# Values of attention: two head groups in one TensorE block, or one group at a time

## The chip, the cores and the metric

The kernel runs on one core of a Trainium2 chip. The metric is the device time of one launch in microseconds (us), the median of three runs. A core has five engines: TensorE (PE, with its weight loads shown apart as PEld), VectorE (DVE), ScalarE (ACT), GpSimd (POOL) and SyncE (SP). Each runs its own list of instructions in a fixed order and waits on semaphores for the others. Matmuls write to PSUM, of which this kernel uses all eight banks of 128 x 512 floats.

## The reference

Attention with normalised queries and keys over 8 batches, 12 heads, 448 tokens and 64 elements a head, and then a multiplicative feed-forward network (FFN) over the 3584 tokens:

```python
q_n, k_n = rmsnorm(q, g_q), rmsnorm(k, g_k)
scores = q_n @ k_n.T / sqrt(64)
attn = exp(scores - max) ; attn = attn / (sum(attn) + 1e-9)
x = (attn @ v) rearranged to [B * S, H * D]          # 3584 x 768
a = x @ w1 ; b = x @ w2                              # 768 -> 1024
out = ((a * b) @ w3) @ w_out                         # 1024 -> 1024 -> 768
```

The kernel leaves the maximum out, multiplies `w3` by `w_out` once (`w34`), and keeps the operands of its matmuls in bf16.

## The kernel before

The 96 heads are handled in 24 groups of four heads (`NQ = 24`, three groups a batch). For group `i` there are:

- preparation: squares on ACT, sums and scaling on DVE, transposition by TensorE (first five groups) or by DMA;
- seven score pieces (`NU = 7`): four 64x64 matmuls into two banks, then one `exp` of 128 x 896 on ACT, which writes `P` (six pieces) or `Pr` (the seventh);
- the values block: three kinds of 16 matmuls each, in 128x32 tiles. Kind 0 multiplies `P` by ones and gives the sums of the softmax, whose reciprocal ACT takes as exp(-ln); kinds 1 and 2 give the values, which DVE multiplies by the reciprocal into `xT`.

When the three groups of a batch are in `xT`, its FFN is pushed on a list as pairs: eight pairs of `x @ w1` or `x @ w2`, and three or four pairs of `(a * b) @ w34`, all in 64x64 tiles. A pair occupies two banks.

No order is written by hand. When the program is built, a planner steps through an estimated time and picks, whenever TensorE is free, what it does next; the order that comes out is fixed in the program. These are the parts that decide about scores and values (`r` is the time less a margin; `idle` are the free banks):

```python
    STOCK = 14
    PACE = 1.7
    # P: three buffers; the third lies in w_outs, once w34 is made
    p_bufs = [const.tile([NP, HQ, NF, S], BF, name="P" + str(z)) for z in range(2)]
    p_bufs.append(w_outs.rearrange("p c n -> p (c n)")[:, 0 : HQ * NF * S]. ...)

    def into(m):                       # DRAIN = 0.11 when the kind of tile changes
        extra = DRAIN if mode[0] != m else 0.0
        mode[0] = m
        return extra

    def score_ready(t):
        ...
        i, g = divmod(n, NU)
        if g == 0 and min(p_free(x) for x in range(3)) > t:
            return False
        stock = sum(p.name != "w" for p in waiting)
        if stock >= STOCK and t < last_score[0] + PACE:
            return False
        return max(qkT_at[i]) + SEM <= t

    def pv_ready(t):
        i = next_pv[0]
        if i >= NQ or all_of(p_at[i], NU) > t or landed[i]["v"] + SEM > t:
            return False
        ...
        if i % 2 or all_of(w34_at, CF) > t or i + 1 >= NQ:
            return True
        return all_of(p_at[i + 1], NU) <= t and landed[i + 1]["v"] + SEM <= t

    def pe_try(t, r):
        idle = idle_banks(r)
        if pv_state:                   # a values block that has begun goes on
            ...
        if mode[0] == "v" and len(idle) >= 1 and pv_ready(r):
            i = next_pv[0]             # the second group follows at once
            took = do_pv_kind(t, i, 0, single(idle))
            pv_state.append((i, 1))
            return took
        two = adjacent(idle)
        score = score_ready(r) and out_scores[0] < 2 and two is not None
        ...                            # the pair that runs goes on; turns; scores
        if late:
            return do_pass(late[0], t)
        want_pv = pv_ready(r)
        if want_pv and len(idle) >= 2:
            i = next_pv[0]
            took = do_pv_kind(t, i, 0, single(idle))
            pv_state.append((i, 1))
            return took
        if two is not None and new is not None and not want_pv:
            waiting.remove(new)
            start_pair(new, two)
            return do_pass(new, t)
```

Once `w34` is complete, an even group's values wait until the scores of the odd group after it have also passed the `exp`; then both groups' values run in one block of 96 matmuls.

Of the kernel before, what the change touches and what calls it, by code (L numbers as in the profile page):

```python
# [9 lines left out]
BF = mybir.dt.bfloat16  # L10
# [10 lines left out]
SEM = 0.05  # L21
# [24 lines left out]
class Planner:  # L46
# [11 lines left out]
    def add(self, *args, **kw):  # L58
        self.jobs.append(Job(*args, **kw))
# [136 lines left out]
def kernel(  # L196
# [15 lines left out]
    B, H, S, D = q.shape  # L212
    NP = 128
# [3 lines left out]
    NF = S // NP  # L217
    NU = 2 * NF + 1
    HQ = 4
    NQB = H // HQ  # L220
    NQ = B * NQB
    DM, DFF = moe_w1.shape
    CM = DM // 128
    CF = DFF // 128
# [5 lines left out]
    const = ctx.enter_context(tc.tile_pool(name="const", bufs=1))  # L230
    prep_pool = ctx.enter_context(tc.tile_pool(name="prep", bufs=3))
    qkT_pool = ctx.enter_context(tc.tile_pool(name="qkT", bufs=3))
    att_pool = ctx.enter_context(tc.tile_pool(name="att", bufs=2))
    p_pool = ctx.enter_context(tc.tile_pool(name="P", bufs=3))
    x_pool = ctx.enter_context(tc.tile_pool(name="x", bufs=3))
    ffn_pool = ctx.enter_context(tc.tile_pool(name="ffn", bufs=4))
    out_pool = ctx.enter_context(tc.tile_pool(name="outp", bufs=3))
# [7 lines left out]
    MARGIN = 0.25  # L245
    AHEAD_W3 = 4
    EARLY = 4
    STOCK = 14
    PACE = 1.7
    POOL_ORDER = (  # L250
        "w0 w1 o0 o1 q1 w2 w3 v0 q2 w4 w5 v1 w6 w7 v2 a0 a1 a2 q3 b0 v3 b1 q4 b2 q5".split()
# [4 lines left out]
    w2s = const.tile([128, CM, DFF], BF, name="w2s")  # L256
    w34s = const.tile([128, CF, DM], BF, name="w34s")
    w_outs = const.tile([128, CF, DM], BF, name="w_outs")
    p_bufs = [const.tile([NP, HQ, NF, S], BF, name="P" + str(z)) for z in range(2)]
    p_bufs.append(  # L260
        w_outs.rearrange("p c n -> p (c n)")[:, 0 : HQ * NF * S].rearrange(
            "p (h j s) -> p h j s", h=HQ, j=NF
        )
    )
    w3s = big_pool.tile([128, CF, DFF], BF, tag="big", name="w3s")
    w3T = big_pool.tile([128, CF, DFF], BF, tag="big", name="w3T")
    g_row = const.tile([1, 2, D], FP, name="g_row")
# [22 lines left out]
    landed = [{"q": INF, "k": INF, "v": INF} for _ in range(NQ)]  # L290
# [5 lines left out]
    p_at = [[] for _ in range(NQ)]  # L296
    pv_end = [INF] * NQ
    x_at = {b: [] for b in range(B)}
    x_used = [INF] * B
# [4 lines left out]
    w34_at = []  # L304
# [5 lines left out]
    def all_of(times, n):  # L310
        return max(times) if len(times) == n else INF
# [243 lines left out]
    mode = ["n"]  # L555

    def into(m):
# [4 lines that stand above are left out]
    def pass_us(n):  # L562
        return n / 2400 + 0.0025

    def idle_banks(t):
        return [z for z in range(8) if bank_at[z] <= t]

    def adjacent(idle):

        fit = [z for z in idle if z + 1 in idle]  # L570
        return min(fit, key=lambda z: (z % 2, z)) if fit else None

    def single(idle):

        return min(idle, key=lambda z: (z ^ 1 in idle, -z)) if idle else None
# [2 lines left out]
    last_score = [0.0]  # L578
    out_scores = [0]

    p_used = [None] * 3

    def p_free(x):

        if p_used[x] is None:
            return 0.0 if x < 2 else all_of(w34_at, CF)
        return pv_end[p_used[x]]

    def score_ready(t):
        n = next_score[0]  # L590
        if n >= NQ * NU:
            return False
        i, g = divmod(n, NU)
        if g == 0 and min(p_free(x) for x in range(3)) > t:
            return False
        stock = sum(p.name != "w" for p in waiting)
        if stock >= STOCK and t < last_score[0] + PACE:
            return False
        return max(qkT_at[i]) + SEM <= t

    def do_score(t, z):
        n = next_score[0]
        next_score[0] += 1
        last_score[0] = t
        i, g = divmod(n, NU)
        s = st[i]
        if g == 0:
            x = min(range(3), key=lambda x: (p_free(x) > t, x))
            s["P"] = p_bufs[x]
            p_used[x] = i  # L610
            s["Pr"] = p_pool.tile([NP, 2, S], BF, tag="Pr", name="Pr")
        took = pass_us(S) + into("n")
        qkT, sc = s["qkT"], ps_all[:, z : z + 2]
        for c in range(2):
            if g < 2 * NF:
                pr, blk = divmod(g, NF)
                j = blk if c == pr else J + blk
            else:
                pr, j = c, NF
            cols = slice(HP * pr, HP * pr + HP)  # L620
            for u in range(2):
                nc.tensor.matmul(  # L622
                    out=sc[HP * c : HP * c + HP, u, 0:S].rearrange(
                        "p (j s) -> p j s", j=NJ
                    ),
                    lhsT=qkT[u * D : (u + 1) * D, 1, j, cols],
                    rhs=qkT[u * D : (u + 1) * D, 0, :, cols],
                    start=True, stop=True, tile_position=(u * D, HP * c),
                )
        dst = (  # L630
            s["P"][:, pr::2, blk, :] if g < 2 * NF else s["Pr"]
        )
        bank_at[z] = bank_at[z + 1] = INF
        out_scores[0] += 1

        def done(e):
            bank_at[z] = bank_at[z + 1] = e + SEM
            out_scores[0] -= 1
            p_at[i].append(e + SEM)

        at = t + took + TO_ENGINE - pass_us(S) + 0.187
        add(
            "ACT", 0.80, QUAD * i + 1.8 * g,
            lambda: nc.scalar.activation(out=dst, in_=sc[:, :, 0:S], func=AF.Exp),  # L644
            needs=[lambda: at - 0.187], done=done,
        )
        if g == NU - 1:
            qkT_used[i] = t + took + 0.2
        return took

    next_pv = [0]
    pv_state = []

    def pv_ready(t):
        i = next_pv[0]
        if i >= NQ or all_of(p_at[i], NU) > t or landed[i]["v"] + SEM > t:
            return False
        b, m = divmod(i, NQB)
        if m == 0 and b >= 3 and x_used[b - 3] > t:
            return False  # L660
        if i % 2 or all_of(w34_at, CF) > t or i + 1 >= NQ:
            return True
        return all_of(p_at[i + 1], NU) <= t and landed[i + 1]["v"] + SEM <= t

    def do_pv_kind(t, i, kind, z):
        s = st[i]
# [354 lines left out]
    def any_turn(t, r, idle, n):  # L1021

        if not idle:
            return None
        if turns:
            i, w = turns[0]
            if scaled_at[i][w] <= r:
                turns.pop(0)
                return do_turn(t, i, w, single(idle))
        ready = [fc for fc in w3_turns if w_at["w3"][fc] + SEM <= r]  # L1030
        if ready and (len(ready) >= n or ready[-1] == CF - 1):
            if ready[0] - len(w34_at) < AHEAD_W3:
                return do_w3_turn(t, w3_turns.pop(0), single(idle))
        return None
# [6 lines left out]
    def pe_try(t, r):  # L1041
        idle = idle_banks(r)
        if pv_state:
            i, kind = pv_state[0]
            z = single(idle)
            if z is None:
                return None
            took = do_pv_kind(t, i, kind, z)
            pv_state.clear()
            if kind == 2:  # L1050
                next_pv[0] += 1
            else:
                pv_state.append((i, kind + 1))
            return took
        if mode[0] == "v" and len(idle) >= 1 and pv_ready(r):
            i = next_pv[0]
            took = do_pv_kind(t, i, 0, single(idle))
            pv_state.append((i, 1))
            return took
        two = adjacent(idle)  # L1060
        score = score_ready(r) and out_scores[0] < 2 and two is not None
        hungry = free["ACT"] <= t + 0.3 and out_scores[0] == 0
        if mode[0] == "t":
            took = any_turn(t, r, idle, 1)
            if took is not None:
                return took
        if running[0] and running[0].ready() <= r:
            if score and hungry:
                return do_score(t, two)
            return do_pass(running[0], t)  # L1070
        took = any_turn(t, r, idle, 2)
        if took is not None:
            return took
        new = next_pair(r)
        late = [p for p in pairs if p.ready() <= r]
        if score:
            left = [z for z in idle if z not in (two, two + 1)]
            if hungry or late or new is None or adjacent(left) is not None:
                return do_score(t, two)
# [12 lines that stand above are left out]
        return any_turn(t, r, idle, 1)  # L1092
# [10 lines left out]
    with tc.manual_schedule():  # L1103
# [66 lines left out]
        for name in POOL_ORDER:  # L1170
            what, x = name[0], int(name[1])
# [9 lines left out]
            else:  # L1181
                dst, src, key = (w1s, moe_w1, "w1") if what == "a" else (w2s, moe_w2, "w2")
# [36 lines left out]
```

## Time and profile before

| what | value |
|---|---|
| time, median of three runs | 363.51 us (362.82 to 363.65) |
| span of the profiled run | 361.6 us |
| TensorE matmuls busy | 348.5 us (96%) |
| weight loads busy | 224.1 us (62%) |
| ACT busy | 265.6 us (73%) |
| DVE busy | 204.1 us (56%) |
| values, 24 groups | 1152 matmuls, 352 ns each, in four singles and ten blocks of two |

A matmul's time in the profile is from its start to the end of its results; matmuls overlap, and four of them run side by side in different tiles. What a matmul costs is read from start to start: a set of four over 448 columns takes 0.189 us, over 384 columns 0.162 us. In a timeline, neighbouring instructions of one kind are merged: the first number is when the group starts, the second how long it lasts, and xN how many instructions it has.

### The profile page before, as it was taken

Reading aid. Unit: us, or ns where it says so; the run is one execution under the profiler, and the core shown is the slowest. Engines: PE = TensorE matmul, PEld = TensorE weight load, DVE = VectorE, ACT = ScalarE, POOL = GpSimd, SP = SyncE. Lnnn points to the kernel's source line nnn. Section 1 sums busy time; section 2 is a strip of 40 time slices with the busy share of each in tenths; the row PEclk is TensorE's granted clock in tenths of the full one; section 3 lists DMA queues with packets and bytes.
Section 4 is the critical chain, followed back from the end, with each engine's and each line's share of the span. In section 5 each row is a group of like instructions: output and inputs, shape, how many; then the busy total and the mean of one; then the engine's idle time right before and its main releaser. Section 6 shows DMA issues by size and latency. Waiting matters only on the chain.

```text
span 361.6 us, 16194 instructions
## 1 busy us (share of the span) xinstructions
PE 348.5 (96%) x7358; PEld 224.1 (62%) x7358; DVE 204.1 (56%) x288; ACT 265.6 (73%) x378; POOL 75.3 (21%) x132
## 2 busy tenths in 40 slices
PE   8789999999999999999999999999999999999984
PEld 3466666557665667666565666655656566666673
DVE  5278367988988788866739497855442311220210
ACT  4879989989999999987998799866974542112121
POOL 8167452400400422040041401305000000000000
PEclk9999999999999999999999999999999999999999
DMA  8999998788999699985499949928530006004115
GB/s 181 255 238 195 262 271 241 144 166 204 240 208 262 109 234 244 222 173 133 103 231 223 168 81 257 203 56 86 98 104 2 4 11 170 4 2 102 37 22 154
DMA packets 68200, 55.11 MB, mean 152 GB/s; under 512 B 44900, under 2 KB 61956, under 8 KB 68132
## 3 DMA queue, kind: packets, MB, share of 16 engines
q1 hardware_dynamic: 49744, 36.51, 43.1%
q0 software_dynamic: 18016, 16.92, 26.8%
q8 instruction: 57, 0.93, 1.1%
q10 hardware_dynamic: 372, 0.66, 0.6%
q14 instruction: 11, 0.09, 0.1%
HBM read 46.66 MB, written 11.01 MB: 159 GB/s over the span
## 4 chain that ended last, share of the span: by engine, by line
PE 90%; DMA 4%; POOL 2%; ACT 2%; issue 1%; DVE 0%; POOLq 0%; DVEq 0%
PE ps_all L758 64%; PE ps_all L675 16%; PE ps_all L622 9%; DMA w3s<-in_moe_w_dram 4%; PE ps_all L976 1%; ACT P L644 1%; PE ps_all L998 1%; ACT w_outs L644 0%; POOL w3s L388 0%; POOL w_outs L394 0%; POOL qk_sb L336 0%; DVE abT L841 0%; POOL v_sb L1118 0%; ACT Pr L644 0%; DVE o_sb L327 0%
## 5 line engine op out<-in xcount | busy, mean ns | idle before, releaser
L644 ACT ACTIVATE P<-ps_all 128x896 bf16<-128x896 f32 x120 | 104.1, 923 | 12.7 <-PE ps_all L622 12.0
L359 POOL DMA_DIRECT2D v_sb<-in_v_dram x96 | 57.1, 611 | 167.5 <-PE ps_all L675 114.2
L758 PE MATMUL ps_all<-xT,w2s 64*64 64x448 bf16 x1536 | 88.5, 349 | 0.1
L758 PE MATMUL ps_all<-xT,w1s 64*64 64x448 bf16 x1536 | 87.3, 349 | 0.0
L758 PE MATMUL ps_all<-w34s,abT 64*64 64x384 bf16 x1792 | 82.3, 323 | 1.3 <-DVE abT L841 1.3
L841 DVE TENSOR_TENSOR abT<-ps_all,a_sb 128x896 bf16<-128x896 f32 x32 | 34.9, 1090 | 78.9 <-PE ps_all L758 69.8
L758 PEld LDWEIGHTS <-abT 64*64 64x64 bf16 x1792 | 57.1, 107 | 18.6 <-issue 1.5
L417 DVE TENSOR_REDUCE ssq<-sq 128x14 f32<-128x896 f32 (+1 forms) x50 | 51.4, 1042 | 23.8 <-ACT sq L410 23.8
L622 PE MATMUL ps_all<-qkT 64*64 64x448 bf16 x672 | 60.2, 352 | 3.1 <-ACT P L644 2.0
L758 PEld LDWEIGHTS <-w2s 64*64 64x64 bf16 x1536 | 46.0, 107 | 26.8 <-POOLq L743 0.5
L758 PEld LDWEIGHTS <-w1s 64*64 64x64 bf16 x1536 | 45.9, 107 | 26.1 <-issue 0.6
L440 DVE TENSOR_TENSOR qks<-qk_sb,al 128x448 bf16<-128x448 f32 x96 | 55.6, 618 | 1.8 <-ACT al L429 1.6
L410 ACT ACTIVATE sq<-qk_sb 128x896 f32<-128x896 f32 (+1 forms) x50 | 45.3, 917 | 1.0 <-DMA qk_sb<-in_q_dram 0.9
L321 ACT ACTIVATE a_sb<-ps_all 128x896 bf16<-128x896 f32 x23 | 21.1, 916 | 28.4 <-PE ps_all L758 28.3
L710 DVE TENSOR_TENSOR xT<-ps_all,r 128x448 bf16<-128x448 f32 x48 | 27.7, 618 | 13.3 <-ACT r L691 13.3
L321 ACT ACTIVATE o_sb<-ps_all 128x768 f32<-128x768 f32 (+1 forms) x19 | 15.2, 798 | 24.6 <-PE ps_all L758 24.6
L622 PEld LDWEIGHTS <-qkT 64*64 64x64 bf16 x672 | 21.4, 106 | 17.9 <-issue 8.4
L675 PEld LDWEIGHTS <-v_sb 128*32 128x32 bf16 x768 | 20.6, 97 | 15.8
L675 PE MATMUL ps_all<-P,v_sb 128*32 128x448 bf16 x480 | 29.6, 352 | 0.0
L644 ACT ACTIVATE w_outs<-ps_all 128x896 bf16<-128x896 f32 x24 | 21.6, 914 | 6.7 <-PE ps_all L622 5.8
L758 PE MATMUL ps_all<-w_outs,w3T 64*64 64x384 bf16 x512 | 24.0, 324 | 0.7 <-DMA w_outs<-in_moe_w_out_dram 0.7
L644 ACT ACTIVATE Pr<-ps_all 128x896 bf16<-128x896 f32 x24 | 22.2, 924 | 3.0 <-PE ps_all L622 3.0
(55 smaller groups left out, 218.4 us busy)
## 6 DMA issues: line engine op xcount, KB each, us to landing
out_dram<-o_sb SPq DMA_DIRECT2D x55, 192.0 KB, 3.8
qk_sb<-in_q_dram SPq DMA_DIRECT2D x18, 448.0 KB, 4.8
qk_sb<-in_k_dram SPq DMA_DIRECT2D x18, 448.0 KB, 5.9
v_sb<-in_v_dram POOLq DMA_DIRECT2D x48, 64.0 KB, 4.8
v_sb<-in_v_dram POOLq DMA_DIRECT2D x48, 48.0 KB, 4.5
qk_sb<-in_q_dram POOLq DMA_DIRECT2D x5, 448.0 KB, 9.1
qk_sb<-in_k_dram POOLq DMA_DIRECT2D x5, 448.0 KB, 9.5
w3s<-in_moe_w_dram POOLq DMA_DIRECT2D x8, 256.0 KB, 5.9
```

Of the source, the lines that this page charges most:

```text
L321: nc.scalar.activation(out=out, in_=in_, func=AF.Copy, scale=1.0 if by is None else by)
L359: nc.gpsimd.dma_start(out=v_bufs[i % 4][p0 : p0 + HP, g::2, 0 : j1 - j0].rearrange("p h j d -> p h (j d)"), in_=src[:, g::2, j0:j1].rearra ...
L410: nc.scalar.activation(out=s["sq", t][:, x0:x1], in_=src[:, t, x0:x1], func=AF.Square)
L417: nc.vector.tensor_reduce(out=s["ssq"][:, t, x0:x1], in_=s["sq", t][:, x0:x1], axis=AX, op=ADD)
L440: nc.vector.tensor_tensor(out=s["qks"][:, t, :, x], in0=src[:, t, x], in1=s["alpha"][:, t, x].unsqueeze(2).broadcast_to([NP, NJ, D]), op=MULT,
L622: nc.tensor.matmul(out=sc[HP * c : HP * c + HP, u, 0:S].rearrange("p (j s) -> p j s", j=NJ), lhsT=qkT[u * D : (u + 1) * D, 1, j, cols], rh ...
L644: lambda: nc.scalar.activation(out=dst, in_=sc[:, :, 0:S], func=AF.Exp),
L675: nc.tensor.matmul(out=ps[hd * HALF : (hd + 1) * HALF, :], lhsT=w, rhs=s["P"][:, hd, j, :] if j < NF else s["Pr"][:, hd // 2, :], start=(j ...
L710: lambda: nc.vector.tensor_tensor(out=xT[b][:, 2 * m + kind - 1, :], in0=ps, in1=s["r"], op=MULT),
L758: mm = nc.tensor.matmul(out=ps_all[64 * h : 64 * h + 64, p.bank + z, 0 : p.n], lhsT=lhsT[64 * r : 64 * r + 64, 64 * h : 64 * h + 64], rhs= ...
L841: nc.vector.tensor_tensor(out=abT[bp][:, f0 : f0 + 2, odd * S : (odd + 1) * S], in0=ps_all[:, z : z + 2, 0:S], in1=a_sb[b, f0], op=MULT,)
L976: nc.tensor.transpose(ps[:, j], s["qks"][:, w, j].rearrange("p x d -> p (x d)"), ident)
```

## The change

The changed kernel gives up the block of two groups. Each group's values run on their own, as soon as its seven `exp` are done and the planner finds a place. The third `P` buffer in `w_outs` goes, `P` comes from a pool of two buffers, and the pool of `Pr` shrinks from three to two with it. The scores of group `i` may begin when the values of group `i - 2` have been taken. The stock of waiting FFN pairs from which scores are paced at 1.7 us falls from 14 to 10. The aim is a simpler order, in which values are taken as they come and `x` of a batch is complete earlier. The arithmetic and the number of matmuls stay the same.

```diff
-    p_pool = ctx.enter_context(tc.tile_pool(name="P", bufs=3))
+    p_pool = ctx.enter_context(tc.tile_pool(name="P", bufs=2))
...
-    STOCK = 14
+    STOCK = 10
...
-    p_bufs = [const.tile([NP, HQ, NF, S], BF, name="P" + str(z)) for z in range(2)]
-    p_bufs.append(
-        w_outs.rearrange("p c n -> p (c n)")[:, 0 : HQ * NF * S].rearrange(
-            "p (h j s) -> p h j s", h=HQ, j=NF
-        )
-    )
...
-    p_used = [None] * 3
-    def p_free(x):
-        if p_used[x] is None:
-            return 0.0 if x < 2 else all_of(w34_at, CF)
-        return pv_end[p_used[x]]
...  # score_ready
-        if g == 0 and min(p_free(x) for x in range(3)) > t:
+        if g == 0 and i >= 2 and pv_end[i - 2] > t:
             return False
...  # do_score
-            x = min(range(3), key=lambda x: (p_free(x) > t, x))
-            s["P"] = p_bufs[x]
-            p_used[x] = i
+            s["P"] = p_pool.tile([NP, HQ, NF, S], BF, tag="P", name="P")
             s["Pr"] = p_pool.tile([NP, 2, S], BF, tag="Pr", name="Pr")
...  # pv_ready
-        if m == 0 and b >= 3 and x_used[b - 3] > t:
-            return False
-        if i % 2 or all_of(w34_at, CF) > t or i + 1 >= NQ:
-            return True
-        return all_of(p_at[i + 1], NU) <= t and landed[i + 1]["v"] + SEM <= t
+        return m > 0 or b < 3 or x_used[b - 3] <= t
...  # pe_try
-        if mode[0] == "v" and len(idle) >= 1 and pv_ready(r):
-            i = next_pv[0]
-            took = do_pv_kind(t, i, 0, single(idle))
-            pv_state.append((i, 1))
-            return took
```

## The prediction

> **What bounds the kernel now.** I read the page's busy times and slices first, then the groups, then the chain in order of time, and last the timeline of TensorE around values blocks and around its few waits.
>
> ```profile
> PE 348.5 (96%) x7358; PEld 224.1 (62%) x7358; DVE 204.1 (56%) x288; ACT 265.6 (73%) x378; POOL 75.3 (21%) x132
> ...
> PE   8789999999999999999999999999999999999984
> ...
> ACT  4879989989999999987998799866974542112121
> PEclk9999999999999999999999999999999999999999
> ```
>
> TensorE is at nine tenths in every slice from the fifth to the last but one, at the full clock. ACT is as full for the first 24 slices (to about 217 us) and then falls off. So two engines are loaded early, TensorE alone late. A busy PE is not yet a PE at its peak, so I checked it by counting. From the groups by shape, in sets of four: 768 sets of the first FFN layer, 168 of scores and 288 of values at 0.189 us, 448 sets of the second layer and 128 for w34 at 0.162 us, 134 transposes at about 0.067 us: 145.2 + 31.8 + 54.4 + 72.6 + 20.7 + 9.0 = 333.7 us of pure streaming in a span of 361.6. The first score set starts at 11.6 us and the last matmul ends 5.4 us ahead of the end. Only about 12 us in between are lost. Taking start-to-start times less streaming, I find 5.5 us of it before 27 us (weights landing), 3.0 us at changes of tile, 1.4 us near 80 us, 0.9 us near 122 us and 1.4 us at 345.7 us. From 123 to 344 us TensorE does not wait once. **The end is set by how much TensorE has to do**, and what the change can win or lose is in the terms of a few microseconds just listed.
>
> The timeline of TensorE around the first block of two groups shows the price of a change of tile:
>
> ```profile
> 86.21 0.98 PE L758 MATMUL ps_all<-w34s,abT 64*64 64x384 bf16 x19
> 87.12 0.75 PE L675 MATMUL ps_all<-P,ones 128*32 128x448 bf16 x12
> 87.69 0.36 PE L675 MATMUL ps_all<-Pr,ones 128*32 128x448 bf16 x4
> 87.88 0.74 PE L675 MATMUL ps_all<-P,v_sb 128*32 128x448 bf16 x12
> ...
> 91.48 0.36 PE L675 MATMUL ps_all<-Pr,v_sb 128*32 128x448 bf16 x4
> 91.77 0.38 PE L622 MATMUL ps_all<-qkT 64*64 64x448 bf16 x4
> 91.98 1.31 PE L758 MATMUL ps_all<-w34s,abT 64*64 64x384 bf16 x28
> ```
>
> Inside the block a set follows the last after 0.19 us (87.69 to 87.88). From the block's last set to the next score it is 91.77 - 91.48 = 0.29 us: 0.10 us too long. At the entry, the last FFN set starts at 86.21 + 0.98 - 0.32 = 86.87 and the values at 87.12: 0.25 us where a set takes 0.16, so 0.09 us. Over all fourteen blocks the sum is 3.0 us, or 0.21 us a block.
>
> The same view before 82 us shows the one cluster of real waits in the middle:
>
> ```profile
> 79.36 0.55 PE L758 MATMUL ps_all<-xT,w2s 64*64 64x448 bf16 x8
> 79.74 0.55 PE L622 MATMUL ps_all<-qkT 64*64 64x448 bf16 x8
> 80.60 0.38 PE L622 MATMUL ps_all<-qkT 64*64 64x448 bf16 x4 [0.31 <-ACT P L644]
> 81.41 0.38 PE L622 MATMUL ps_all<-qkT 64*64 64x448 bf16 x4 [0.43 <-ACT P L644]
> 81.60 1.17 PE L758 MATMUL ps_all<-w34s,abT 64*64 64x384 bf16 x24
> ```
>
> The first FFN layer of batch 0 has ended at 79.7; its second layer can start only when DVE has made the last products; nothing is left but scores, and each score waits for an exp to free its banks. The groups show what one such wait is made of:
>
> ```profile
> L644 ACT ACTIVATE P<-ps_all 128x896 bf16<-128x896 f32 x120 | 104.1, 923 | 12.7 <-PE ps_all L622 12.0
> ```
>
> Scores can't come faster than one every 0.8 to 0.9 us, against 0.19 us of TensorE: three of them in a row lose 1.4 us. The same thing happens at 121.4 to 123.1 (0.9 us).
>
> **What the Trainium skill says.** "TensorEngine Tiling (Array Packing)", section Key Properties: changing the tiling mode, and not just the tile, drains TensorE. The trace agrees: about 0.10 us at each change between 64x64 and 128x32, nothing extra within one mode. "TensorE: Matmul & The Clock Gate", section "Wait — 56ns, not 53.3ns?": a warm matmul follows the last after N / 2.4 GHz plus some 2.5 ns; for 448 columns that is 189.2 ns, and the trace has 189. "Perfetto Trace Analysis", section Identifying the Most-Contended Engine, warns that matmul busy time is a bad measure, which is why I counted sets above rather than trust 96%.
>
> **The change part by part.**
>
> 1. *Blocks split.* The 24 groups are now in four singles and ten blocks of two, so 14 blocks. Afterwards nothing joins two groups, as the branch that let a second group follow at once is gone and a pass or a score will come between. That makes 24 blocks, ten more, each with one more entry and one more exit: 10 x 0.21 = **+2.1 us**, all on TensorE. Ahead of 123 us there are two or three of these, where they may fall into waits; the other seven or eight (1.5 to 1.7 us) hit a TensorE that never waits. I count the whole 2.1. A transpose ahead of values costs much the same at the entry (0.149 us start to start, of which 0.067 is streaming), so it is no matter what stands before a block.
>
> 2. *Values no longer wait for the partner.* An even group's values become ready about one group of scores, 7 to 15 us, sooner. Group 4 has its last score at 74.3 and its values only at 87.1; group 8 at 120.1 and 130.7. A values block is 12 x 0.189 = 2.27 us of work that needs no scarce ACT result, and is larger than each of the waits at 80 (1.4 us) and 122 us (0.9). If it falls there, both go: -2.3 us. But the planner takes ready values before it starts a new pair, so group 4's may be spent at 76 or 77 us, ahead of the hole, which then comes two microseconds later with the same shape. I give it a bit under half: **-0.9 us**. Batch 2 also has its x at about 124 instead of 135, which helps to refill the list; later the list is never empty, so nothing is won there.
>
> 3. *Two P buffers, not three.* The scores of group i + 2 now wait for the values of i. They were ready a whole group earlier, and a pair that runs delays them by at most some 2 to 5 us, less than the 7 exps of one group need (7 x 0.92 = 6.4 us). ACT may wait now and then, which matters only while TensorE has no stock, before 123 us. Up to 78 us the kernel before has only two buffers too (the third is in w_outs), with ACT 24.3 of 26 us busy from 52 to 78; between 92 and 118 it was 25.25 of 26. That 4% over some 40 us is 1.5 us of exp time, of which a part can return as wait: **+0.3 us**.
>
> 4. *STOCK 10.* A batch adds 11 or 12 pairs, two of which start at once. So scores are paced at 1.7 us a little after each push, and more once stock remains. It moves exps later, from where ACT is full to where it is half empty. From 291 us on TensorE has nothing but 64 us of FFN, so attention may end tens of microseconds later with no harm. **0 us**.
>
> 5. *Start and end.* The first 27 us don't touch the changed branches (no values before 27.1 us). The wait of 1.3 us for the last product at 345.7 and the 5.4 us after the last matmul belong to the order of the last batch, which stays: **0 us**.
>
> Sum: +2.1 - 0.9 + 0.3 = +1.5 us, 363.5 + 1.5 = **365.0 us**, 0.4% slower.
>
> **The rivals.** (a) *The holes are filled and all else stays*: 363.5 + 2.1 - 2.3 = 363.3 us. For it: the first values fit into the very hole at 80 us. Against it: the planner's preference for values ahead of new pairs. (b) *ACT becomes the bound early*: with two buffers and a lower stock, scores slow down, the FFN list runs dry at each batch's end, and a hole like that at 80 us (1 to 1.5 us) appears at two or three more batches: 363.5 + 2.1 + 3 = 368.6 us. For it: ACT at nine tenths to 217 us, and only two holes' distance from empty. Against it: values are never later, so the FFN of each batch is pushed sooner. (c) *The switches are hidden*, since values beside idle gaps cost nothing: then only the gains count and the time is 362 to 363 us. Against it: no wait at all between 123 and 344 us to hide them in.
>
> **Range and chances.** The low end takes all of the hole's gain and a little better refill (362.6); the high end takes the full switches, no gain and one more hole (367.8). All three rivals lie within 1.5%; 2% is 7.3 us, three times the switch cost, so a change by over 2% either way needs something I don't see. Faster 0.01, same 0.96, slower 0.03.
>
> **What would show it right or wrong.** In the timeline after: 24 blocks of 48 matmuls at line of the values matmul, each with about 0.09 us at entry and 0.10 at exit (step 1); no wait of TensorE for ACT's P near 80 and 122 us, or the same holes a few microseconds later (step 2); ACT's busy share from 92 to 118 us below 97% (step 3); the last values later than 288.5 us with fewer than 64 us of FFN after them (step 4); the wait for the last product still about 1.3 us (step 5). The prediction is wrong if blocks still abut, if TensorE waits in the stretch from 123 to 344 us, or if the final FFN is broken up by scores.

## The result, and the profile after

The changed kernel takes 366.88 us (median of six runs, 366.32 to 367.98); the kernel before took 363.06 beside it. The ratio is 1.0106, with a 95% interval from 1.0087 to 1.0126: 3.8 us, or 1.1%, slower. The ratios given here can differ by up to 0.0007 from the quotient of the two medians. The profiled run is the longest of the six, with 367.98 us and a span of 366.2.

The page of the changed kernel, busy times and slices:

```profile
PE 352.2 (96%) x7358; PEld 220.9 (60%) x7358; DVE 207.7 (57%) x292; ACT 264.7 (72%) x374; POOL 75.4 (21%) x132
...
PE   8799999999889999999999999999999999999984
...
ACT  4879989959969999997688669976796557122221
PEclk9999999999999999999999999999999999999999
```

Same number of matmuls, same clock, but TensorE now shows two slices of eight tenths (the 11th and 12th, 92 to 110 us), and ACT has dips to five and six tenths at the ninth and twelfth slice, where it had eight and nine.

TensorE around 80 us, where the kernel before waited 1.4 us (its timeline):

```profile
77.17 1.87 PE L738 MATMUL ps_all<-xT,w2s 64*64 64x448 bf16 x36
78.97 0.75 PE L655 MATMUL ps_all<-P,ones 128*32 128x448 bf16 x12
...
81.06 0.36 PE L655 MATMUL ps_all<-Pr,v_sb 128*32 128x448 bf16 x4
81.36 0.38 PE L606 MATMUL ps_all<-qkT 64*64 64x448 bf16 x4
81.57 1.47 PE L738 MATMUL ps_all<-w34s,abT 64*64 64x384 bf16 x32
```

Group 4's values stand exactly in the old hole: nothing waits, and the exit of the block costs 81.36 - 81.06 = 0.30 us, as before. But the hole comes back ten microseconds later. The same view from 91 us:

```profile
91.07 0.67 PE L606 MATMUL ps_all<-qkT 64*64 64x448 bf16 x8
92.17 0.38 PE L606 MATMUL ps_all<-qkT 64*64 64x448 bf16 x4 [0.42 <-ACT P L628]
92.48 0.75 PE L655 MATMUL ps_all<-P,ones 128*32 128x448 bf16 x12
...
94.86 0.38 PE L606 MATMUL ps_all<-qkT 64*64 64x448 bf16 x4
95.18 0.75 PE L655 MATMUL ps_all<-P,ones 128*32 128x448 bf16 x12
96.44 0.37 PE L655 MATMUL ps_all<-Pr,ones 128*32 128x448 bf16 x4 [0.51 <-ACT Pr L628]
...
102.36 1.30 PE L738 MATMUL ps_all<-xT,w2s 64*64 64x448 bf16 x22
105.11 0.38 PE L738 MATMUL ps_all<-xT,w2s 64*64 64x448 bf16 x2 [1.46 <-issue]
```

The FFN of batch 0 is used up at 91 us, and batch 1 is not complete; a score waits for an exp, then the values of group 6, which the plan begins ahead of their last exp, wait for it. The last two lines are something else: TensorE stops after 22 matmuls of 24, in the middle of a set of four, and waits for nothing that the profile shows. More on that below.

To compare kernels I take, for each stretch, its length less the pure streaming of the matmuls in it (0.189 us a set over 448 columns, 0.162 over 384, 0.056 a transpose). That is TensorE's lost time, in us:

| stretch | before | changed, first trace | changed, second trace |
|---|---|---|---|
| 0 to 78 | 11.9 | 11.8 | 11.7 |
| 78 to 90 (old hole at 80) | 1.5 | 0.3 | 0.3 |
| 90 to 98 (new hole) | 0.3 | 2.1 | 2.1 |
| 98 to 118 | 0.2 | 2.6 | 1.1 |
| 118 to 136 | 1.2 | 1.3 | 1.5 |
| 136 to 340 | 1.9 | 3.6 | 3.5 |
| the last wait, at 346 or 350 | 1.5 | 1.5 | 1.5 |
| sum | 18.5 | 23.1 | 21.6 |

The lower part is plain: from 136 us to the last wait nothing stops for more than 0.15 us in either kernel, and the changed one loses 1.6 to 1.7 us more; it has seven more blocks there, 7 x 0.21 = 1.5 us. The upper part needed experiments. (The columns and their sums are rounded one by one.)

### The profile page after: what moved, and what is told of

Its sections match the earlier page's. It is cut to its first block, busy times and chain, and to the rows that moved or that the text cites. A ratio compares the mean times of both kernels' runs of the same rounds, so it can differ in the third digit from the quotient of the medians.

```text
span 366.2 us, 16186 instructions
## 1 busy us (share of the span) xinstructions
PE 352.2 (96%) x7358; PEld 220.9 (60%) x7358; DVE 207.7 (57%) x292; ACT 264.7 (72%) x374; POOL 75.4 (21%) x132
## 4 chain that ended last, share of the span: by engine, by line
PE 93%; ACT 4%; DVE 1%; issue 1%; DVEq 0%; ACTq 0%
PE ps_all L738 65%; PE ps_all L655 15%; PE ps_all L606 9%; ACT P L628 2%; PE ps_all L1096 2%; PE ps_all L956 1%; PE ps_all L978 1%; DVE abT L821 1%; ACT w3T L315 1%; ACT sq L404 0%; ACT Pr L628 0%; ACT w34s L315 0%; DVE qkT L321 0%; ACT r L671 0%; DVE o_sb L321 0%
## 5 line engine op out<-in xcount | busy, mean ns | idle before, releaser
L628 ACT ACTIVATE P<-ps_all 128x896 bf16<-128x896 f32 x144 | 127.5, 917 | 33.4 <-PE ps_all L606 30.9
L738 PE MATMUL ps_all<-xT,w1s 64*64 64x448 bf16 x1536 | 90.0, 349 | 0.2 <-issue 0.2
L738 PE MATMUL ps_all<-w34s,abT 64*64 64x384 bf16 x1792 | 81.3, 323 | 1.3 <-DVE abT L821 1.3
L738 PEld LDWEIGHTS <-abT 64*64 64x64 bf16 x1792 | 54.2, 107 | 21.5 <-issue 1.9
L738 PEld LDWEIGHTS <-w1s 64*64 64x64 bf16 x1536 | 47.0, 107 | 25.5 <-issue 1.0
L315 ACT ACTIVATE a_sb<-ps_all 128x896 bf16<-128x896 f32 x20 | 18.3, 917 | 24.1 <-PE ps_all L738 24.0
L655 PE MATMUL ps_all<-P,v_sb 128*32 128x448 bf16 x576 | 35.7, 352 | 0.0
L315 ACT ACTIVATE o_sb<-ps_all 128x768 f32<-128x768 f32 (+1 forms) x18 | 14.2, 791 | 20.1 <-PE ps_all L738 19.9
L321 DVE COPY o_sb<-ps_all 128x768 f32<-128x768 f32 (+1 forms) x11 | 10.1, 920 | 26.6 <-PE ps_all L738 24.3
```

The source lines that it names most:

```text
L315: nc.scalar.activation(out=out, in_=in_, func=AF.Copy, scale=1.0 if by is None else by)
L321: nc.vector.tensor_copy(out=out, in_=in_)
L655: nc.tensor.matmul(out=ps[hd * HALF : (hd + 1) * HALF, :], lhsT=w, rhs=s["P"][:, hd, j, :] if j < NF else s["Pr"][:, hd // 2, :], start=(j ...
L738: mm = nc.tensor.matmul(out=ps_all[64 * h : 64 * h + 64, p.bank + z, 0 : p.n], lhsT=lhsT[64 * r : 64 * r + 64, 64 * h : 64 * h + 64], rhs= ...
```

## The experiments

**The changed kernel again.** No edit. The second trace was wanted because a stop without a semaphore may belong to one launch.

> The changed kernel once more, with nothing altered. Its trace stops for 1.5 us in the middle of a set of four matmuls near 104 us and again for 0.2 us near 111.5, with no semaphore to wait for. If that stop belongs to this order of instructions (TensorE's next instructions come late because transfers are dense there), it is seen again within 1 us of the same place, and the time is 366 to 368 us. If it is an accident of one launch, the stretch from 98 to 112 us loses under 0.5 us instead of 2.3, and the span is 364 to 365 us.

Measured: 366.41 us, ratio 1.008 (1.0053 to 1.0106), span 364.6; a fourth run, of 371.96 us at a lower granted clock (0.987 instead of 0.996 to 0.999), is left out. Where the first trace lost 1.6 us in a stop (1.46 of them idle), this one loses 0.4, at the same two matmuls:

```profile
103.84 0.38 PE L738 MATMUL ps_all<-xT,w2s 64*64 64x448 bf16 x2 [0.23 <-issue]
```

The hole at 91 to 97 us is the same within 0.01 us (2.1 us from 90 to 98). So the size of the stop depends on the launch, and the hole belongs to the order. The span of 364.6 is 3.0 us over the 361.6 of before; the other 1.6 us of the first trace are the larger stop and a second one at 111.6 us. What the traces show of the stop: TensorE's instructions come in packets of 16,384 bytes on a queue of their own, 57 in all, one for every 256 of its instructions. In the first trace one starts at 90.5 us and the next only at 102.8, 12.3 us later, where about 6 is usual; in the kernel before the same two lie at 90.9 and 98.3. "Runtime: NRT & Kernel Launch", section Instruction fetch mechanics, says that instructions are refilled in 16 KiB blocks by DMA, mostly hidden. The trace agrees on size and on "mostly"; it also shows a refill that was not. That the stop is a wait for such a packet can be seen by its place: counted in TensorE's list of instructions, all nine stops of this kind in the traces of this case (over 0.1 us, after 27 us) lie a multiple of 256 instructions apart, and each ends 1.3 to 1.5 us after the last packet has ended. Why the packet came late was not settled. Transfers are dense there (the DMA share is 1.06 from 100 to 118 us), but they are in the kernel before too (1.20); and in the second trace, where the stop cost 0.4 us, the gap between the two packets was 11.6 us, hardly shorter than 12.3.

**The price of a change of tile, alone.** The kernel before, order untouched, with one small matmul in the other tile between the two groups of each block:

```diff
         if mode[0] == "v" and len(idle) >= 1 and pv_ready(r):
             i = next_pv[0]
-            took = do_pv_kind(t, i, 0, single(idle))
+            z = single(idle)
+            nc.tensor.matmul(
+                out=ps_all[0:64, z, 0:64], lhsT=warm_t[0:64, 0:64],
+                rhs=warm_t[0:64, 0:64], start=True, stop=True,
+                tile_position=(0, 0), skip_group_check=True,
+            )
+            took = do_pv_kind(t, i, 0, z)
```

The next matmuls overwrite its result, so the output is the same.

> The kernel before, order unchanged, with one tiny 64x64 matmul (64 columns) put between the two groups of each of the ten blocks, so that the tile changes twice more in each: the price of the split blocks by itself. If a change of tile costs 0.10 us whatever surrounds it, the time rises by 10 x (0.20 + about 0.03 for the matmul) = 2.0 to 2.5 us, all inside the ten blocks. If TensorE's later waits absorb it, or if the drains overlap, it rises by under 1 us.

Measured: 365.68 us against 363.55, ratio 1.0055 (1.0035 to 1.0075): +2.1 us. Its timeline in the first block:

```profile
88.27 0.36 PE L675 MATMUL ps_all<-Pr,v_sb 128*32 128x448 bf16 x4
88.56 0.21 PE L1058 MATMUL ps_all<-warm_t 64*64 64x64 bf16 x1
88.71 0.75 PE L675 MATMUL ps_all<-P,ones 128*32 128x448 bf16 x12
```

From the last set of one group to the first of the next it is 88.71 - 88.27 = 0.44 us, where within a block it is 0.19: two drains and a matmul of 64 columns cost 0.25 us. Over the trace, 28 changes in or out of values cost 3.03 us in the kernel before (0.108 each), and 48 changes cost 5.19 us here. Ten blocks more are 2.1 us, as the prediction had it. (The ten small matmuls are in the measured 2.1 us too, with some 0.03 us each, an estimate from 0.189 us for 448 columns; that is within the noise.)

**The split alone.** Pairing removed, everything else as before:

```diff
-        if i % 2 or all_of(w34_at, CF) > t or i + 1 >= NQ:
-            return True
-        return all_of(p_at[i + 1], NU) <= t and landed[i + 1]["v"] + SEM <= t
+        return m > 0 or b < 3 or x_used[b - 3] <= t
...
-        if mode[0] == "v" and len(idle) >= 1 and pv_ready(r):
-            ...   # the second group follows at once
```

> The kernel before with the pairing alone removed (values of a group run as soon as they are ready), with three P buffers and the stock of 14 as before. Theory one (the split costs the switches, and the rest of the changed kernel's loss is the accident of where TensorE runs dry between 91 and 112 us): +2.1 us less the hole at 80 us of 1.2, so 364 us, if no new hole opens. Theory two (two P buffers hold back the scores): also 364 us, and the two buffers make the other 3 us. Theory three (the values taken one by one upset the early order whatever the buffers): 366 to 367 us, with a hole between 90 and 112 us here too.

Measured: 366.00 us against 363.55, ratio 1.0066 (1.0045 to 1.0087): +2.45 us. That is the time of theory three, but the new hole at 91 us that was to cause it is not there. The old one at 80 us is, two microseconds later (1.5 us lost from 78 to 84), and so is that near 122 (1.0). So splitting costs the switches in full and wins nothing back; the gain of 1.2 us that I had put down to it is missing.

**The changed kernel with the old stock.**

```diff
-    STOCK = 10
+    STOCK = 14
```

> The changed kernel with the stock of 14 put back. If the lower stock costs nothing, as the prediction says, 366 to 368 us; the order up to 105 us should be nearly the same since few pairs wait there. If pacing scores at a stock of 10 caused the hole near 91 to 97 us, that hole goes and the time is 364 to 365 us.

Measured: 365.59 us (365.42 to 365.77), ratio 1.0055 (1.0035 to 1.0074): 0.8 us less than the changed kernel beside it, with no run of the one within the runs of the other. The hole at 91 to 97 us goes and the old one is back, at 83 us:

```profile
76.91 0.75 PE L655 MATMUL ps_all<-P,ones 128*32 128x448 bf16 x12
...
79.29 0.57 PE L606 MATMUL ps_all<-qkT 64*64 64x448 bf16 x8
...
83.28 0.38 PE L606 MATMUL ps_all<-qkT 64*64 64x448 bf16 x4 [0.45 <-ACT P L628]
84.09 0.38 PE L606 MATMUL ps_all<-qkT 64*64 64x448 bf16 x4 [0.43 <-ACT P L628]
84.28 5.39 PE L738 MATMUL ps_all<-w34s,abT 64*64 64x384 bf16 x128
```

It is the shape of before, two to three microseconds later: group 4's values were taken at 76.9 us, ahead of the hole. This kernel differs from the split alone in its two P buffers only, and is 0.4 us faster, so two buffers cost nothing here. The 0.4 us are not a gain of the buffers as such: in this order two pairs of blocks happen to adjoin (from 257 and from 294 us), so there are 44 changes of tile instead of 48, and 4 x 0.108 = 0.4.

Why the stock matters is read from TensorE's timeline from 52 us on, when batch 0 puts its 11 pairs on the list. The scores of group 3 before:

```profile
53.08 0.36 PE L622 MATMUL ps_all<-qkT 64*64 64x448 bf16 x4
...
53.43 0.36 PE L622 MATMUL ps_all<-qkT 64*64 64x448 bf16 x4
...
54.75 0.36 PE L622 MATMUL ps_all<-qkT 64*64 64x448 bf16 x4
...
56.24 0.36 PE L622 MATMUL ps_all<-qkT 64*64 64x448 bf16 x4
```

and in the changed kernel:

```profile
52.70 0.36 PE L606 MATMUL ps_all<-qkT 64*64 64x448 bf16 x4
...
54.88 0.39 PE L606 MATMUL ps_all<-qkT 64*64 64x448 bf16 x4
...
56.85 0.39 PE L606 MATMUL ps_all<-qkT 64*64 64x448 bf16 x4
...
58.56 0.39 PE L606 MATMUL ps_all<-qkT 64*64 64x448 bf16 x4
```

What follows from it is best compared with the stock of 14 above, the same kernel otherwise. Group 3's last score comes at 62.3 us instead of 60.0, and group 4's last exp ends at 77.0 instead of 75.7. Group 4's values therefore start at 79.0 instead of 76.9, which puts them into the old hole, and group 5's scores start behind them, at 81.4 instead of 79.3. By then the second layer of batch 0 is ready (81.57 in the timeline above), so its matmuls stand between group 5's scores, which take 6.3 us instead of 4.8; the last, the one that batch 1 waits for, comes at 87.7 instead of 84.1. Group 5's values start at 92.5 instead of 89.6, and the FFN of batch 0 is used up at 91.

It is not that ACT as a whole falls behind. From 52 to 92 us it is busy for 34.3 us instead of the 37.4 of the kernel before, but it ends 23 exps there instead of 21; what it does less of are squares, copies and reciprocals. By 78 us both have ended 35 exps; by 83 us the changed kernel has 36 and the kernel before 40. The delay is in the order, at group 5.

Not all of the 0.8 us is the hole. Against the stock of 14, the second trace of the changed kernel loses 0.5 us more from 78 to 98 us; the stop of 0.4 us and four more changes of tile (0.4) are in the difference too, and it loses 0.4 us less before 78.

**A stock of 10 with the blocks of two.** The kernel before, with `STOCK = 10` as its only edit.

> The kernel before with its blocks of two and three P buffers, and only the stock lowered from 14 to 10. If a lower stock is harmless, as the prediction has it, 363.5 us. If pacing scores at a stock of 10 lets TensorE run dry between two batches (as it seemed to do in the changed kernel near 91 to 97 us), new waits of 1 to 3 us appear before 140 us and the time is 365 to 367 us.

Measured: 367.11 us against 363.25, ratio 1.0109 (1.0088 to 1.0129): +3.9 us, all from one number. Its timeline has the hole at the same place, and one more at a batch's end at 213 us, where the kernel before never waits:

```profile
95.24 0.76 PE L622 MATMUL ps_all<-qkT 64*64 64x448 bf16 x12
96.87 0.38 PE L622 MATMUL ps_all<-qkT 64*64 64x448 bf16 x4 [0.86 <-ACT Pr L644]
97.69 0.57 PE L758 MATMUL ps_all<-xT,w1s 64*64 64x448 bf16 x8 [0.45 <-DVE xT L710]
...
213.11 0.36 PE L622 MATMUL ps_all<-qkT 64*64 64x448 bf16 x4
214.62 1.66 PE L758 MATMUL ps_all<-w34s,abT 64*64 64x384 bf16 x36 [1.15 <-POOLq L743]
```

POOLq is the semaphore with which one half of a pair hands its bank to the other; with nothing else to do, TensorE waits for it.

**The split with a stock of 10 and three P buffers.** The edits of the split and `STOCK = 10`.

> Pairing removed and the stock at 10, but three P buffers kept: the changed kernel in all but its buffers. If two buffers hold scores back, 365.5 us or less. If the buffers do nothing once values are taken one group at a time, the same as the changed kernel, 366.5 us, with the values blocks at the same places.

Measured: 367.67 us (366.62 to 368.75), ratio 1.0123 (1.0096 to 1.0151), span 364.1. TensorE's matmuls come in the same order as in the changed kernel for the first 5542 of 7358 (to 275 us), so the third buffer changes nothing until the last quarter. The new hole is there (2.05 us from 90 to 98). Whether the 1 us between this and the changed kernel is more than scatter can't be told from four runs.

**Two P buffers with the blocks of two.** The other part alone:

```diff
-        if g == 0 and min(p_free(x) for x in range(3)) > t:
+        if g == 0 and min(p_free(x) for x in range(2)) > t:
...
-            x = min(range(3), key=lambda x: (p_free(x) > t, x))
+            x = min(range(2), key=lambda x: (p_free(x) > t, x))
```

> The kernel before with blocks of two, but only two P buffers: no scores of the next pair until the first group of a block has been read. If ACT's lead matters, it idles for some 5 us at each block and TensorE runs dry early: 365 us or more. If TensorE's stock of FFN covers it, ACT loses time and TensorE does not: 363.5 to 364 us.

Measured: 364.10 us against 363.25, ratio 1.0030 (1.0019 to 1.0041): +0.9 us. Blocks of two need the third buffer a little; it has one more wait, of 1.4 us at 208 us, for the same hand-over, against which its last wait is 0.7 us shorter.

**When the lower stock does its harm.** The changed kernel, with the limit in force in one part of the plan: first early only, then late only.

```diff
-        if stock >= STOCK and t < last_score[0] + PACE:
+        if stock >= (STOCK if t < 90.0 else 14) and t < last_score[0] + PACE:   # early
+        if stock >= (14 if t < 90.0 else STOCK) and t < last_score[0] + PACE:   # late
```

> The changed kernel with the stock of 10 in force only while the planner's time is under 90 us, and 14 after that. Theory one: a stock of 10 does its harm at the first batch, where it spaces group 3's scores 2.0 us apart, ACT falls behind by some 3 us up to 92 us, and TensorE runs dry before batch 1 is ready. Then the waits at 91 to 98 us stay and the time is that of the changed kernel, 366.5 us. Rival: the harm comes from pacing in the middle, where ACT is full too; then the time is 365.6 us as with 14 throughout.

> The counterpart: a stock of 14 while the planner's time is under 90 us, 10 after that. Theory one: 365.6 us, as with 14 throughout, and scores of group 3 come as fast as in the kernel before (53.0, 53.4, 54.7, 56.2 us). Rival: a new wait opens at a later batch, before TensorE has its backlog (123 us), and the time is 366.5 us.

Measured: 367.61 us (ratio 1.0108, 1.0084 to 1.0132) and 367.20 us (ratio 1.0108, 1.0076 to 1.0140). Theory one holds for the first: the hole from 90 to 98 us is there with 2.1 us. It fails for the second: group 3's scores are quick again (52.7, 53.0, 54.4, 55.8 us) and that hole is gone, but the time is no better. The late kernel keeps the old hole (1.5 us at 82) and loses more later: 1.36 us from 160 to 200 us against 0.71 in the changed kernel's second trace, and 1.8 at the end. So a stock of 10 does harm both early and late, and the two harms do not add up. That each takes the place of another wait is seen for the early one (the hole at 91 instead of that at 82); for the late one it is argued, not shown. The early kernel also has a stop in mid-set like that of the changed kernel (0.9 us at 104.9).

**Blocks of three.** The opposite direction, a whole batch in one block from group 6 on, 11 blocks instead of 14:

```diff
-    STOCK = 14
+    STOCK = 13
+    BLOCK_ENDS = (0, 1, 2, 3, 5, 8, 11, 14, 17, 20, 23)
...
-        if i % 2 or all_of(w34_at, CF) > t or i + 1 >= NQ:
-            return True
-        return all_of(p_at[i + 1], NU) <= t and landed[i + 1]["v"] + SEM <= t
+        last = next(x for x in BLOCK_ENDS if x >= i)
+        return all(
+            all_of(p_at[x], NU) <= t and landed[x]["v"] + SEM <= t
+            for x in range(i + 1, last + 1)
+        )
```

> The opposite direction: from group 6 on, the three groups of a batch run their values in one block (11 blocks in all, where the kernel before has 14), with the three P buffers of before and a stock of 13. If the price is 0.21 us a block and nothing else moves, 3 x 0.21 = 0.6 us less than before: 362.9 us, and some 0.4 less if the waits at 80 or 122 us shrink. If holding three groups back starves ACT of buffers (all three P are full when a block starts) and this reaches TensorE, waits appear at scores after each block and the time is 364 us or more.

Measured: 362.95 us against 363.25, ratio 0.9992 (0.9976 to 1.0009): not told apart from the kernel before. In the trace the 22 changes cost 2.37 us where 28 cost 3.03, so the 0.66 us are there, and the hole at 122 us is gone (0.1 us lost from 118 to 124 instead of 1.0); the span is 360.3 us. The runs, from 361.4 to 364.6, scatter by more than this.

**Blocks of three, and the last wait.** All the traces above but two (blocks of two with a stock of 10, and with two P buffers) lose 1.5 to 1.8 us between 344 and 351 us, most of it in a wait for the last product of the last batch. The edit keeps one ready pair for that moment:

```diff
         bp, odd = divmod(b, 2)
+        if b == B - 1:
+            held = [p for p in waiting if p.name == "o"][-1:]
+            for p in held:
+                waiting.remove(p)
+            waiting.extend(held)
         waiting.extend(
             ffn2_pair(bp, t) for t in (...)
```

> Blocks of three from group 6 on with a stock of 13, as in the run of that kind, and one more change: a pair of the second FFN layer whose inputs are long ready is kept for the end, ahead of the last batch's second layer, where every kernel here waits 1.3 us for the last product. The pair takes 2.6 us of TensorE, more than the wait, so the wait goes: 1.3 us less than the blocks of three alone, 361.6 us. If the wait only moves (another product late), 362.5 us or more.

Measured: 360.87 us against 363.45, ratio 0.9935 (0.9912 to 0.9957): 2.6 us less than the kernel before and some 6 less than the changed one. The end of TensorE's first layer and its second layer now abut:

```profile
340.82 1.11 PE L761 MATMUL ps_all<-xT,w2s 64*64 64x448 bf16 x20
341.76 4.56 PE L761 MATMUL ps_all<-w34s,abT 64*64 64x384 bf16 x104
```

The span falls by 1.2 us from that of the blocks of three, the size of the wait.

## Why the prediction was right, and where it was not

The time of 366.88 us lies within 362.6 to 367.8, but 1.9 us above the 365.0. The main mechanism was right: TensorE sets the end, and the changes of tile are paid in full. Of the 3.0 us by which the second trace is longer than that of before, they make 2.3 us (5.3 instead of 3.0); the hole that moved makes 0.6 (2.4 us instead of 1.8 from 78 to 98), the stop 0.4, and ahead of 78 us it loses 0.2 less. The high end of the range was reckoned as full switches, no gain and one more hole, which is close to what came. By its steps:

1. **Blocks split, +2.1 us: right.** Measured alone it is +2.1 us, and 48 changes of tile are counted where 28 were. No two blocks abut in the changed kernel.
2. **Values no longer wait, -0.9 us: wrong, and by size the largest miss; the split alone wins nothing (+2.45 us in all, 2.1 of them the switches).** The step's own doubt came true: with the stock left at 14, ready values are taken ahead of a new pair, at 75.9 us (76.9 with two buffers), and the hole follows with the same shape. Rival (a), the hole filled, can be seen in the changed kernel's timeline, but there only because scores come later, and the 1.2 us saved at 80 are lost at 91 (1.8).
3. **Two P buffers, +0.3 us: the sign was wrong for the split, and the size small either way.** It is 365.59 against 366.00 us, with four changes of tile fewer by chance of the order. Where blocks of two remain, two buffers cost 0.9 us.
4. **Stock of 10, 0 us: wrong in its mechanism.** It costs 0.8 us in the split kernel and 3.9 us in the kernel before. I looked at where pacing moves the exps to in the end (where ACT has room) and not at the first place where it bites: at 52 us it delays group 3's scores, and through groups 4 and 5 batch 1's last values come 2.9 us later, when batch 0's FFN has run out. This is the empty list of rival (b), but with the stock as its cause and not the buffers, and without ACT as the bound.
5. **Start and end, 0 us: right.** 11.9 and 11.7 us of loss up to 78 us; the last wait is 1.27 us in both.

Step 2 missed by 1.25 us, step 3 by 0.7 the other way and step 4 by 0.8; that the last two nearly cancel is luck. From 363.55 us the measured terms lead to 363.55 + 2.45 - 0.4 + 0.8 = 366.4, but only because each is the difference of two neighbouring kernels. In another order they are others: from 363.25, the stock first is +3.9, and the split on top of it +0.6.

Two readings in the prediction are loose. A transpose streams for 0.056 us, not 0.067, so its sum of streaming is 1.5 us too high; and ACT has slices of seven tenths within the first 24, so it was not full throughout.

Of the signs named ahead: ACT's share from 92 to 118 us fell below 97% (21.98 of 26 us), and the last values came at 309.1 us instead of 288.5. TensorE did wait once more after 123 us, 0.8 us at 125 to 126, which the prediction had named as a sign of being wrong. It stands where the hole of before at 122 us (0.9) would be, three microseconds later; after it nothing of more than 0.15 us comes before the end.

## What to carry to other kernels

Where TensorE streamed without waits, each change of tile shape was paid in full (0.108 us here), so blocks that need another shape are worth joining, as far as TensorE does not run dry for it. A limit that delays scores must be judged at the first place where it bites, and followed from there to the next batch, not by where the work lands in the end. A busy sum can mislead there: ACT did less in all from 52 to 92 us, and yet more exps. And filling one hole is no gain until the next place where the supply runs out has been looked at.

## What was not expected of the hardware

TensorE can stop in the middle of a set of four matmuls without a semaphore: 1.6 us are lost in one trace, 0.3 to 0.9 us in three others at about the same place (102 to 105 us). The stops lie a multiple of 256 instructions apart and end 1.3 to 1.5 us after a packet of instructions has, so they are waits for instructions. In the traces of the changed kernel, of the stock that is lowered early and of the split with a stock of 10 and three P buffers, the gap between two packets there is 10.8 to 12.3 us, where 6 is usual; the loss at that place is 1.6, 0.4, 0.9 and nothing, so the gap alone does not decide it. None of the traces of the kernel before or of the blocks of three has one over 0.3 us there. The cause of the lateness stays open.
